# Linear attention and two MLPs in one kernel: keys, values and `q` loaded ahead of most weights, weight conversions in another order, six of them moved from the end of stage one into the slots

## The chip, the core and the metric

The kernel runs on one core of a Trainium2 chip. The metric is the device time of one execution in microseconds (us). Engines: PE is TensorE, DVE VectorE, ACT ScalarE, POOL GpSimd; SP is the queue that issues most DMAs.

## What is computed

A linear attention with RMS normalisation over 8 x 8 heads of 576 tokens, then two MLPs on its 4608 x 512 output, all in float32. The weights arrive as float64 and are read as pairs of 32-bit words.

```python
kv = einsum('bhsd,bhse->bhde', k, v); out = einsum('bhsd,bhde->bhse', q, kv)
x = out / sqrt(mean(out * out, -1) + 1e-6) * g_norm      # then (4608, 512)
x = square(maximum(x @ w_in, 0)) @ w_out                 # moe,  512 -> 2048 -> 512
h = x @ w_in2;  out = (h * cos(h)) @ w_out2              # moe2, 512 -> 2048 -> 512
```

## The kernel before

**Numbers.** A float32 operand is split in a high and a low part (`xh`, `xl`; `wh`, `wl`; `gh`, `gl`), and a product takes three matmuls: high by high, high by low, low by high. ACT rounds the high part, DVE or POOL subtracts it from the value.

**Weights.** `load_w` brings a block of float64 words (512 KB) to SBUF as a tile `raw`, `conv_steps` makes float32 of it. Kind "one" is one block of `w_in` (i = 0) or `w_out` (i = 1) of the first MLP and stays in SBUF as high and low part: six instructions on DVE (L119, L121, L124 in `words`, L130, L133 in `value`, L208) and two on ACT (L120, L207). Kinds "pair" and "seven" take four blocks, add four sums and differences of them in the `raw` tile itself (L177), keep seven, split these (L189 on ACT, L191 on DVE) and write both parts to HBM (`wi_d`, `ws_d`), 448 KB each; only when the second of these DMAs (`wi_d<-raw`, L194) has landed is the `raw` tile free. There are two such tiles (`conv_p`, `bufs=2`); blocks of kind "one" with i = 1 use two tiles of another pool.

**Stage one** takes the first half of the first MLP's 2048 columns in 72 chunks (nine tiles of 512 tokens by eight column blocks f): `layer_in` (L385, 12 matmuls), `act_relu2` (ACT: L394 relu, L395 square, L396 high part; DVE: L397 low part `gl`), and two chunks later `layer_out` (L419, 12 matmuls). Beside it runs the attention: `kv_mm` (L264), `att_a` (L294, L298), `att_b` (L320 and following), `att_c` and `att_d` on DVE, up to chunk 49. The first two batches' attention goes straight into the tiles of the first chunks. Chunks 0 and 1 need the blocks (0, 0) and (1, 0); chunk f needs (f, 0), and its `layer_out` (f, 1).

**The slots**, 30 of them, follow stage one. A slot is one tile of up to 1024 tokens by one group of column blocks: ten slots (0 to 9) for the rest of the first MLP, twenty for the second. They do their products by a scheme of seven block products out of eight (`first_product` L507, `second_product` L669, `second` L606), with weights that the conversions left in HBM (loads `wi`, `ws`, `wo` from SP).

**The order of the side work** is a table of due times, `jobs`, in units of chunks and slots: `at(n, fn, ...)`. `w_items` and `w_at` hold the conversions and when each begins; `Stream.place` spreads a conversion's steps behind its begin (the tuples `steps`, in chunks, or in slots for n of nA0 = 72 and more) and loads a later block when one is done. `pos(s)` is slot s. From chunk 50 to chunk 65 fourteen conversions stand (eight pairs of the first MLP, six of the second), in the slots 1 to 7 another fourteen. A scheduler then orders the instructions on each engine, once, by its own estimates; engines and SP work through their lists in order.

Of the kernel before, what the change touches and what calls it, by code (L numbers as in the profile page):

```python
# [12 lines left out]
AF = mybir.ActivationFunctionType  # L13
ALU = mybir.AluOpType
# [8 lines left out]
def kernel(  # L23
# [15 lines left out]
    nc = tc.nc  # L39
# [3 lines left out]
    NH = NF // 2  # L43
    NP = NH // 2
    NEXACT = 2
    NQ = 3
# [5 lines left out]
    D = 64  # L52
# [17 lines left out]
    gcol = cpool.tile([P, 1], F32, name="gcol")  # L70
# [12 lines left out]
    seven = {(0, 0)} | {(1, q) for q in range(NP)}  # L83
# [20 lines left out]
    def as32(ap):  # L104
        return ap.bitcast(F32)

    def temp(shape, dtype, name):
        return pools["t"].tile(shape, dtype, tag="t", name=name)
# [28 lines left out]
    def load_w(kind, m, f, i):  # L137
        if kind == "seven":
            raw = conv_p.tile([P, 4, P, 2], U32, tag="raw", name="raw")
            for df, places in ((0, (1, 0)), (1, (2, 3))):  # L140
                src = (wA, wB)[m][2 * f + df, :, 1, :].rearrange("p (c n) -> p c n", n=2 * P)
                for d, place in enumerate(places):
                    nc.sync.dma_start(out=raw[:, place].rearrange("p n two -> p (n two)"), in_=src[:, 2 * d + i, :])
        elif kind == "pair":
            raw = conv_p.tile([P, 4, P, 2], U32, tag="raw", name="raw")
            for df, dst in ((0, raw[:, 1:3]), (1, raw[:, 0::3])):
                src = (wA, wB)[m][2 * f + df, :, 0, :].rearrange("p (c n) -> p c n", n=2 * P)
                nc.sync.dma_start(out=dst.rearrange("p k n two -> p k (n two)"), in_=src[:, i::2, :])
        else:
            if kind == "one" and i:  # L150
                raw = x_p.tile([P, DM, 2], U32, tag="xr", name="raw", bufs=2)
            else:
                raw = conv_p.tile([P, DM, 2], U32, tag="raw", name="raw")
            nc.sync.dma_start(out=raw.rearrange("p n two -> p (n two)"), in_=(wA, wB)[m][f, :, i, :])
        raws[kind, m, f, i] = raw
# [123 lines left out]
    def load_q(b, p):  # L279
        t = att_p.tile([P, S], F32, tag="q", name="q", bufs=NQ)  # L280
        nc.sync.dma_start(out=t, in_=qT[p * P:(p + 1) * P, b * S:(b + 1) * S])
        q_sb[b, p] = t
# [89 lines left out]
    gs = {}  # L372
# [3 lines left out]
    def layer_in(t, *fs):  # L376

        pss = [bank("l") for _ in fs]
        for c in range(NKC):
            xh, xl = xs[t, c]  # L380
            cs = slice(c * P, (c + 1) * P)
            for f, ps in zip(fs, pss):
                wh, wl = wts[0, f]
                for k, (a, m) in enumerate(((wh, xh), (wh, xl), (wl, xh))):
                    nc.tensor.matmul(  # L385
                        ps, a[:, 0, cs], m[:], start=(c == 0 and k == 0), stop=(c == NKC - 1 and k == 2)
                    )
        return pss

    def act_relu2(ps):  # L390
        r, g = (temp([P, TOK], F32, n) for n in "rg")
        h = g_p.tile([P, TOK], F32R, tag="gh", name="gh")
        l = g_p.tile([P, TOK], F32R, tag="gl", name="gl")
        nc.scalar.activation(out=r, in_=ps, func=AF.Relu)  # L394
        nc.scalar.activation(out=g, in_=r, func=AF.Square)  # L395
        nc.scalar.copy(out=h, in_=g)  # L396
        nc.vector.tensor_tensor(out=l, in0=g, in1=as32(h[:]), op=ALU.subtract)  # L397
        return h, l
# [307 lines left out]
    chunks = [(t, f) for t in range(NTILE) for f in range(NH)]  # L706
    nA0 = NTILE * NH
    nAtt = 49
# [3 lines left out]
    def at(n, fn, *a):  # L712
        jobs.append((n, len(jobs), fn, a))

    def pos(slot):
        return nA0 + slot + 0.002

    class Stream:
# [10 lines left out]
        def place(self, positions, after, skip=()):  # L729
            for k, (n, item) in enumerate(zip(positions, self.items)):  # L730
                steps = (0, 0.06, 0.13, 0.3, 0.45)
                if n < nA0:
                    steps = (0, 0.25, 0.5, 0.75, 1.0, 1.25, 1.4) if n < nAtt else (0, 0.15, 0.3, 0.5, 1.0)
                if self.use != conv_w or item[0] == "one":
                    at(n, self.use, *item)
                    steps = (after,)
                for d in steps[:-1]:
                    at(n + d, conv_part, *item)
                if k not in skip:
                    at(n + steps[-1], self.advance)  # L740

    def outs_of(m, ps):
        return [("out", m, f, 1) for p in ps for f in (2 * p, 2 * p + 1)]

    def pairs_in(m, ps, kind="pair"):
        return [(kind, m, p, i) for p in ps for i in range(2)]

    w_items, w_at = [], []
    for fs, n, step in ((range(2), -14, 0.1), (range(2, 6), -2.2, 0.7), (range(6, NH), 4, 0.8)):
        new = [("one", 0, f, i) for f in fs for i in range(2)]  # L750
        w_items += new
        w_at += [n + step * k for k in range(len(new))]
    for new, n0, n1 in (
        (pairs_in(0, range(4, 6), "seven") + outs_of(0, range(6, 8)) + pairs_in(1, range(6, 8), "seven") + pairs_in(1, range(4), "seven"), 13, nAtt + 1),
        (pairs_in(0, range(NP, 2 * NP)) + pairs_in(1, range(3)), nAtt + 1, nA0 - 7),
        (pairs_in(1, range(3, 2 * NP)) + pairs_in(1, range(4, 6), "seven"), pos(1), pos(7)),
    ):
        w_items += new
        w_at += [n0 + (n1 - n0) / len(new) * k for k in range(len(new))]
    w_stream = Stream(load_w, conv_w, w_items)  # L760
    w_stream.place(w_at, 0.5, range(2 * NH - NRAW, 2 * NH - NRAW + 2))

# [4 lines left out]
    for b, (s0, ds) in enumerate(starts):  # L767
        for i, u in enumerate(att_units(b)):
            n = s0 + i * ds
# [51 lines left out]
    def run_jobs(n):  # L821
        nonlocal done
        while done < len(jobs) and jobs[done][0] <= n:
            _, _, fn, a = jobs[done]
            done += 1
            fn(*a)

    def run_chunks(lo, hi):
        for n in range(lo, hi):
            if n < LAG:  # L830
                if n == 0:
                    first = layer_in(0, *range(LAG))
                    banks["l"] = ["l0"]
                ps = first[n]
            else:
                ps, = layer_in(*chunks[n])
            gs[chunks[n]] = act_relu2(ps)
            run_jobs(n)
            if n >= LAG:
                layer_out(*chunks[n - LAG])  # L840
            run_jobs(n + 0.5)
# [40 lines left out]
        run_jobs(here)  # L882

    for j in range(2):
        nc.sync.dma_start(out=gcol[j * D:(j + 1) * D, :], in_=g_norm.rearrange("(d o) -> d o", o=1))
    nc.vector.memset(epsb, EPS)
    nc.scalar.activation(out=zerob, in_=epsb, func=AF.Abs_reciprocal_sqrt)
    nc.vector.memset(zerob, 0.0)
# [6 lines left out]
    with ExitStack() as early:  # L895
        pools["ps"] = early.enter_context(tc.tile_pool(name="ps0", bufs=1, space=PSUM))
        def right(name, bufs):
            return early.enter_context(tc.tile_pool(name=name, bufs=bufs, side="right"))

        right("pad", 1).tile([P, 56], F32, name="pad")  # L900
        x_p, g_p, ev_p, pools["t"] = (right(n, b) for n, b in (("x", XB), ("g", 3), ("ev", 2), ("tmp", 8)))
        with tc.tile_pool(name="att", bufs=1, side="right") as att_p:
            kvx = [att_p.tile([P, NKC, P], F32, tag=f"kvx{b}", name=f"kvx{b}") for b in range(2)]
            for x in kvx:
                nc.gpsimd.memset(x, 0.0)
            w_stream.advance(2)
            kv_stream.advance(KVB)
            w_stream.advance(NRAW - 2)
            for p in range(NQ):
                load_q(0, p)  # L910
            run_jobs(-1)
            banks.update(o=["o", "l1"], ss=["ss"], l=["l0", "acc3"])
            run_chunks(0, nAtt)
        pools["x"] = ctx.enter_context(tc.tile_pool(name="xb", bufs=13, side="left"))
        banks["l"] = ["l0", "l1", "o", "ss"]
        run_chunks(nAtt, nA0)
        for c in chunks[-LAG:]:
            layer_out(*c)
# [47 lines left out]
```

## Time and profile before

| | us |
|---|---|
| median of 3 runs (1587.4 to 1589.66) | 1588.98 |
| the profiled execution | 1588.0 |
| its span, first to last instruction | 1586.2 |
| PE busy | 1552.5 (98%) |
| DVE busy | 1243.9 (78%) |
| ACT busy | 1073.7 (68%) |

Stage one takes the span up to 507 us, the slots the rest. A busy PE is not a PE at its peak: matmuls overlap, and their ends are modelled. Matmuls of 128 x 512 that follow each other without a wait start 0.23 us apart, and each is shown as some 0.39 us long. Where PE waits for short times or its clock is lowered, the number of matmuls in a window shows it better than the busy time. A row of a table of windows reads: begin and end, length, busy us (instructions) of PE, of PEld (weight loads), DVE, ACT and POOL, granted TensorE clock, busy share of the 16 DMA engines, GB/s. In a timeline a row reads: start, us, engine, line, instruction, its tiles, shapes, and in brackets the engine's idle time before it and what ended it.

### The profile page before, as it was taken

How to read it: one execution, taken by the hardware profiler on the slowest of the kernel's cores; microseconds unless marked ns; L12 is line 12 of the kernel's file. 1: busy time of each engine (PE TensorE's matmuls, PEld its weight loads, DVE VectorE, ACT ScalarE, POOL GpSimd, SP SyncE). 2: the span in 40 equal slices, each digit the busy share in tenths (PEclk: the TensorE clock that was granted, in tenths of full speed). 3: DMA queues.
4: the chain of work that ended last, by engine and by line, in shares of the span. 5: the costliest groups of instructions: out<-in, count | busy, mean ns of one | idle time of the engine just before them, and what ended most of it. 6: DMA issues, size and time to landing. Idle time of an engine off the chain costs nothing.

```text
span 1586.2 us, 24792 instructions
## 1 busy us (share of the span) xinstructions
PE 1552.5 (98%) x9164; PEld 1359.8 (86%) x9164; DVE 1243.9 (78%) x1688; ACT 1073.7 (68%) x1535; POOL 116.4 (7%) x125
## 2 busy tenths in 40 slices
PE   5999999999989999999999999999999999999998
PEld 4777777778777878888999899999999999999998
DVE  7977868798766798888747678967896788689677
ACT  5977768775545755555636667776777677777774
POOL 1100211111100000000000000000000001100110
PEclk9999999999999999999999999999999999999999
DMA  8855978777679989999987678988999889999995
GB/s 320 276 157 163 279 225 248 217 212 225 213 221 333 320 263 340 312 345 304 339 273 288 231 215 270 269 260 262 268 264 280 239 259 287 279 365 308 265 363 170
DMA packets 236951, 425.53 MB, mean 268 GB/s; under 512 B 18464, under 2 KB 155168, under 8 KB 236832
## 3 DMA queue, kind: packets, MB, share of 16 engines
q1 hardware_dynamic: 225840, 387.78, 72.9%
q0 software_dynamic: 10992, 36.18, 11.3%
q8 instruction: 73, 1.20, 0.3%
q14 instruction: 46, 0.38, 0.1%
HBM read 309.85 MB, written 80.22 MB: 246 GB/s over the span
## 4 chain that ended last, share of the span: by engine, by line
PE 83%; DVE 6%; DMA 5%; issue 3%; ACT 2%; SPq 0%; POOL 0%; DVEq 0%; ACTq 0%; POOLq 0%
PE FA L507 15%; PE FB L507 15%; PE SA L669 13%; PE SB L669 12%; PE acc L419 9%; PE l L385 9%; PE SB L606 3%; PE SA L606 3%; DMA wi_d<-raw 1%; DMA raw<-in_wB 1%; DMA sum<-part 1%; DMA q<-in_qT 1%; DVE raw L177 1%; ACT wh L189 1%; DMA raw<-in_wA 1%
## 5 line engine op out<-in xcount | busy, mean ns | idle before, releaser
L507 PE MATMUL FA<-xh,wi 128*128 128x512 f32 (+1 forms) x840 | 306.1, 370 | 1.1 <-ACT ev L405 0.9
L507 PE MATMUL FB<-xh,wi 128*128 128x512 f32 (+1 forms) x840 | 306.1, 370 | 0.0
L669 PE MATMUL SB<-ws,gh 128*128 128x256 f32 x1008 | 237.9, 280 | 1.1 <-ACT u L521 0.8
L669 PE MATMUL SA<-ws,gh 128*128 128x256 f32 x1008 | 237.9, 280 | 0.0
L669 PEld LDWEIGHTS SB<-ws,gh 128*128 128x128 f32 x1008 | 185.9, 188 | 14.4 <-ACT u L521 1.0
L669 PEld LDWEIGHTS SA<-ws,gh 128*128 128x128 f32 x1008 | 186.2, 188 | 13.2
L507 PEld LDWEIGHTS FA<-xh,wi 128*128 128x128 f32 x840 | 157.8, 188 | 11.0 <-ACT ev L405 1.3
L507 PEld LDWEIGHTS FB<-xh,wi 128*128 128x128 f32 x840 | 157.8, 188 | 8.2
L646 DVE TENSOR_TENSOR gl<-y,gh 128x1024 fp32r<-128x1024 f32 (+1 forms) x100 | 111.4, 1114 | 39.1 <-ACT gh L645 38.9
L669 PE MATMUL SA<-ws,gl 128*128 128x256 f32 x504 | 141.0, 280 | 1.1 <-DVE gl L646 1.1
L669 PE MATMUL SB<-ws,gl 128*128 128x256 f32 x504 | 141.2, 280 | 0.8 <-DVE gl L646 0.8
L695 POOL DMA_DIRECT2D sum<-part x71 | 60.3, 850 | 1100.8 <-ACT part L694 1082.2
L566 DVE SCALAR_TENSOR_TENSOR y<-y,h 128x1024 f32<-128x1024 f32 (+1 forms) x80 | 89.2, 1115 | 53.6 <-ACT y L562 53.2
L548 ACT ACTIVATE y<-h,zerob 128x1024 int32<-128x1024 f32 (+1 forms) x80 | 85.1, 1064 | 50.7 <-DVE h L527 50.7
L419 PE MATMUL acc<-gh,wh 128*128 128x512 f32 x288 | 114.5, 399 | 4.2 <-ACT gh L396 2.5
L419 PE MATMUL acc<-gl,wh 128*128 128x512 f32 x288 | 114.4, 397 | 2.1 <-DVE gl L397 2.1
L419 PE MATMUL acc<-gh,wl 128*128 128x512 f32 x288 | 113.6, 395 | 0.0
L507 PE MATMUL FA<-xl,wi 128*128 128x512 f32 (+1 forms) x300 | 111.0, 370 | 0.0
L507 PE MATMUL FB<-xl,wi 128*128 128x512 f32 (+1 forms) x300 | 110.9, 370 | 0.0
L669 PEld LDWEIGHTS SB<-ws,gl 128*128 128x128 f32 x504 | 94.7, 188 | 7.9 <-DVE gl L646 1.5
L669 PEld LDWEIGHTS SA<-ws,gl 128*128 128x128 f32 x504 | 94.7, 188 | 7.8 <-DVE gl L646 1.3
L645 ACT CAST gh<-y 128x1024 fp32r<-128x1024 f32 (+1 forms) x100 | 94.5, 957 | 6.1 <-DVE y L628 6.0
(178 smaller groups left out, 3781.6 us busy)
## 6 DMA issues: line engine op xcount, KB each, us to landing
wi<-wi_d SPq DMA_DIRECT2D x210, 512.0 KB, 6.9
ws<-ws_d SPq DMA_DIRECT2D x175, 512.0 KB, 5.8
sum<-part POOLq DMA_DIRECT2D x45, 512.0 KB, 7.7
kvld<-in_kv SPq DMA_DIRECT2D x32, 512.0 KB, 6.9
wi_d<-wh SPq DMA_DIRECT2D x24, 448.0 KB, 4.1
wi_d<-raw SPq DMA_DIRECT2D x24, 448.0 KB, 4.0
raw<-in_wA SPq DMA_DIRECT2D x20, 512.0 KB, 5.5
wo<-wo_d SPq DMA_DIRECT2D x20, 512.0 KB, 6.4
```

The source lines that it names most:

```text
L177: nc.vector.tensor_tensor(out=a[:, o], in0=a[:, x], in1=a[:, y], op=op)
L189: nc.scalar.copy(out=h, in_=a[:, lo:end])
L385: nc.tensor.matmul(ps, a[:, 0, cs], m[:], start=(c == 0 and k == 0), stop=(c == NKC - 1 and k == 2))
L419: nc.tensor.matmul(o, a[:, cs], m[:], start=(f == 0 and n == 0), stop=(f == NH - 1 and n == 2), skip_group_check=True)
L507: nc.tensor.matmul(ps[:, pp, :], a, b, start=(i in (0, 1, 2) and n == 0), stop=(n == 5), skip_group_check=True)
L548: nc.scalar.activation(out=y.bitcast(I32), in_=hs[k, b], func=AF.Identity, bias=zerob)
L566: nc.vector.scalar_tensor_tensor(out=y, in0=y, scalar=-2.0 * math.pi, in1=hs.pop((k, b)), op0=ALU.add, op1=ALU.mult)
L606: nc.tensor.matmul(ps, lhs, rhs, start=(a == 0 and (x, y) == (0, 0)), stop=last, skip_group_check=True)
L645: nc.scalar.copy(out=h, in_=src)
L646: nc.vector.tensor_tensor(out=l, in0=src, in1=as32(h), op=ALU.subtract)
L669: nc.tensor.matmul(ps[:, b, :], lhs, rhs, start=(i in (0, 1, 2) and n == 0 and (m == 0 or b % 2 == 0)), stop=(n == 5), skip_group_check=True,)
L695: nc.gpsimd.dma_start(out=e, in_=part, accum_op=ALU.add)
```

## The change

- `g_norm` is loaded by POOL's queue, not by SP's. SP's first loads are one weight block, the five blocks of keys and values of batch 0, `q` of the first head pair, and then weights and `q` in turn; before, two weight blocks came first and two more ahead of all `q`.
- The sixteen blocks of kind "one" are converted in another order: (0, 0), (1, 0), (2, 0), (0, 1) ahead of the first chunk, then block (f, 0) 3.4 chunks and block (f, 1) 0.7 chunks ahead of chunk f. Before: 0 to 3, both halves in turn, ahead of the first chunk, then 4 to 7.
- Six conversions (the first three pairs of the second MLP) move from the end of stage one to the slots, where twenty now stand from slot 1 to slot 9.2. Those that stay have their steps 0.25 chunks apart, over 1.4 chunks in all, before over 1.0.
- From chunk 49 on the square of `act_relu2` is made by DVE from PSUM, max(ps, 0) times the relu, not by ACT.

```diff
             else:
-            if kind == "one" and i:
+            if kind == "one" and w_items.index((kind, m, f, i)) % 4 > 1:
                 raw = x_p.tile([P, DM, 2], U32, tag="xr", name="raw", bufs=2)
...
-    def act_relu2(ps):
+    def act_relu2(ps, busy):
...
-        nc.scalar.activation(out=g, in_=r, func=AF.Square)
+        if busy:
+            nc.scalar.activation(out=g, in_=r, func=AF.Square)
+        else:
+            nc.vector.scalar_tensor_tensor(out=g, in0=ps, scalar=0.0, in1=r, op0=ALU.max, op1=ALU.mult)
...
                 if n < nA0:
-                    steps = (0, 0.25, 0.5, 0.75, 1.0, 1.25, 1.4) if n < nAtt else (0, 0.15, 0.3, 0.5, 1.0)
+                    steps = (0, 0.25, 0.5, 0.75, 1.0, 1.25, 1.4)
...
-    for fs, n, step in ((range(2), -14, 0.1), (range(2, 6), -2.2, 0.7), (range(6, NH), 4, 0.8)):
-        new = [("one", 0, f, i) for f in fs for i in range(2)]
-        w_items += new
-        w_at += [n + step * k for k in range(len(new))]
+    ones_at = {(0, 0): -14, (1, 0): -13.9, (2, 0): -4, (0, 1): -3}
+    for f in range(NH):
+        ones_at.setdefault((f, 0), f - 3.4 if f > 2 else 0)
+        ones_at.setdefault((f, 1), f - 0.7)
+    for (f, i), n in sorted(ones_at.items(), key=lambda x: x[1]):
+        w_items.append(("one", 0, f, i))
+        w_at.append(n)
...
-        (pairs_in(0, range(NP, 2 * NP)) + pairs_in(1, range(3)), nAtt + 1, nA0 - 7),
-        (pairs_in(1, range(3, 2 * NP)) + pairs_in(1, range(4, 6), "seven"), pos(1), pos(7)),
+        (pairs_in(0, range(NP, 2 * NP)), nAtt + 1, nA0 - 7),
+        (pairs_in(1, range(2 * NP)) + pairs_in(1, range(4, 6), "seven"), pos(1), pos(9.2)),
...
-            gs[chunks[n]] = act_relu2(ps)
+            gs[chunks[n]] = act_relu2(ps, n < nAtt)
...
-        nc.sync.dma_start(out=gcol[j * D:(j + 1) * D, :], in_=g_norm.rearrange("(d o) -> d o", o=1))
+        nc.gpsimd.dma_start(out=gcol[j * D:(j + 1) * D, :], in_=g_norm.rearrange("(d o) -> d o", o=1))
...
-            w_stream.advance(2)
+            w_stream.advance(1)
             kv_stream.advance(KVB)
+            load_q(0, 0)
+            w_stream.advance(1)
+            load_q(0, 1)
             w_stream.advance(NRAW - 2)
-            for p in range(NQ):
-                load_q(0, p)
+            load_q(0, 2)
```

In the orders below line numbers of the changed kernel differ: `gl` is L400 there (before L397), the moved square L398.

SP at the program's start, before (`raw` are weight blocks, `kvld` keys and values):

```order
L885 DMA gcol<-in_g_norm 64x1 x2
L154 DMA raw<-in_wA 128x1024 x2
L252 DMA kvld<-in_kv 128x1024 x4
L252 DMA kvld<-in_kv 64x1024
L154 DMA raw<-in_wA 128x1024 x2
L281 DMA q<-in_qT 128x576 x3
```

SP at the same place, now:

```order
L154 DMA raw<-in_wA 128x1024
L252 DMA kvld<-in_kv 128x1024 x4
L252 DMA kvld<-in_kv 64x1024
L281 DMA q<-in_qT 128x576
L154 DMA raw<-in_wA 128x1024
L281 DMA q<-in_qT 128x576
L154 DMA raw<-in_wA 128x1024 x2
L281 DMA q<-in_qT 128x576
```

`gcol` and the second weight block have left the place ahead of the keys and values, and the first `q` stands right behind these.

DVE from the fourth conversion's first instruction to the first instruction of attention, L335, before:

```order
L119 TENSOR_SCALAR e<-raw 128x512
L133 SCALAR_TENSOR_TENSOR w<-w,e 128x512
L121 TENSOR_SCALAR w<-raw 128x512
L130 SCALAR_TENSOR_TENSOR e<-raw,e 128x512
L208 TENSOR_TENSOR wl<-w,wh 128x512
L124 SCALAR_TENSOR_TENSOR w<-raw,w 128x512
L133 SCALAR_TENSOR_TENSOR w<-w,e 128x512
L119 TENSOR_SCALAR e<-raw 128x512
L335 SCALAR_TENSOR_TENSOR m<-ss,r_311 128x288
```

DVE from the second conversion's first instruction to the first instruction of attention, now:

```order
L119 TENSOR_SCALAR e<-raw 128x512
L121 TENSOR_SCALAR w<-raw 128x512
L124 SCALAR_TENSOR_TENSOR w<-raw,w 128x512
L130 SCALAR_TENSOR_TENSOR e<-raw,e 128x512
L133 SCALAR_TENSOR_TENSOR w<-w,e 128x512
L335 SCALAR_TENSOR_TENSOR m<-ss,r_287 128x288
```

Ahead of attention's first instruction stood four conversions, the last one still without its L208, and the beginning of a fifth; now there are two, the second without its L208.

DVE near the end of stage one, one conversion and the `gl` around it, before:

```order
L397 TENSOR_TENSOR gl<-g,gh 128x512
L191 TENSOR_TENSOR raw<-raw,wh 128x896
L119 TENSOR_SCALAR e<-raw 128x512
L121 TENSOR_SCALAR w<-raw 128x512
L124 SCALAR_TENSOR_TENSOR w<-raw,w 128x512
L130 SCALAR_TENSOR_TENSOR e<-raw,e 128x512
L133 SCALAR_TENSOR_TENSOR raw<-w,e 128x512
L177 TENSOR_TENSOR raw<-raw 128x128 x4
L397 TENSOR_TENSOR gl<-g,gh 128x512
L191 TENSOR_TENSOR raw<-raw,wh 128x896
```

DVE at the same place, now:

```order
L400 TENSOR_TENSOR gl<-g,gh 128x512
L398 SCALAR_TENSOR_TENSOR g<-l_4888,r 128x512
L119 TENSOR_SCALAR e<-raw 128x512
L121 TENSOR_SCALAR w<-raw 128x512
L400 TENSOR_TENSOR gl<-g,gh 128x512
L124 SCALAR_TENSOR_TENSOR w<-raw,w 128x512
L130 SCALAR_TENSOR_TENSOR e<-raw,e 128x512
L133 SCALAR_TENSOR_TENSOR raw<-w,e 128x512
L177 TENSOR_TENSOR raw<-raw 128x128 x4
L398 SCALAR_TENSOR_TENSOR g<-o,r 128x512
L191 TENSOR_TENSOR raw<-raw,wh 128x896
L400 TENSOR_TENSOR gl<-g,gh 128x512
```

A conversion now spans two `gl` where it spanned one, and each chunk's square stands on DVE as well.

## Rows read from the trace of the kernel before

**Rows 1.** The page, part 1: busy us, share of the span, instructions.

```profile
PE 1552.5 (98%) x9164; PEld 1359.8 (86%) x9164; DVE 1243.9 (78%) x1688; ACT 1073.7 (68%) x1535; POOL 116.4 (7%) x125
```

**Rows 2.** Windows, end of stage one: length, busy us (count) by engine, clock, DMA.

```profile
360.00:400.00 40.00, 40.00 (x178) 33.10 (x178) 32.37 (x64) 23.27 (x39) 4.02 (x3) 1.00 0.72 220
400.00:440.00 40.00, 38.33 (x168) 30.96 (x167) 31.29 (x60) 20.64 (x34) 4.56 (x3) 1.00 0.69 213
440.00:480.00 40.00, 35.40 (x142) 27.68 (x141) 29.27 (x60) 21.15 (x33) 0.00 (x0) 0.91 0.80 245
```

**Rows 3.** Timeline of PE, 455 to 483 us: start, us, instruction [idle before, releaser].

```profile
467.58 0.79 PE L419 MATMUL acc<-gl,wh 128*128 128x512 f32 x1 [1.43 <-DVE gl L397]
```

**Rows 4.** Timeline of DVE, 465 to 478 us.

```profile
471.93 0.43 DVE L119 TENSOR_SCALAR e<-raw 128x512 uint32<-128x512 uint32 x1 [3.61 <-DMA raw<-in_wB]
...
475.67 0.69 DVE L397 TENSOR_TENSOR gl<-g,gh 128x512 fp32r<-128x512 f32 x1
```

**Rows 5.** Chain of waits, 395 to 485 us: start, us, what.

```profile
426.10 3.22 DMA wi_d<-raw
...
429.76 3.43 DMA raw<-in_wB
...
439.77 3.21 DMA wi_d<-raw
```

**Rows 6.** Timeline of SP at the start.

```profile
0.74 1.23 SPq L885 DMA_DIRECT2D gcol<-in_g_norm  x2
```

**Rows 7.** Timeline of PE at the start.

```profile
18.54 2.26 PE L294 MATMUL acc<-q,kvx 128*128 128x288 f32 x4 [1.79 <-DMA q<-in_qT]
```

**Rows 8.** Windows of the start.

```profile
0.00:25.00 25.00, 11.88 (x97) 9.07 (x98) 14.60 (x34) 10.59 (x22) 1.19 (x6) 1.00 0.88 322
...
50.00:95.00 45.00, 44.77 (x274) 34.15 (x273) 44.77 (x98) 38.71 (x87) 4.22 (x7) 1.00 0.67 217
```

**Rows 9.** Windows, instructions of DVE on tile `raw` alone (then clock, DMA share, GB/s).

```profile
400.00:440.00 40.00, 26.97 (x52) 1.00 0.69 213
```

**Rows 10.** Windows of slots: 6 to 9, ten us, slots 9, 3, 7, 10.

```profile
720.90:848.20 127.30, 127.30 (x694) 121.78 (x693) 90.17 (x106) 69.44 (x86) 0.00 (x0) 1.00 0.91 318
770.00:780.00 10.00, 10.00 (x60) 10.00 (x59) 10.00 (x12) 7.08 (x10) 0.00 (x0) 1.00 1.03 403
818.50:848.20 29.70, 29.70 (x174) 29.70 (x173) 26.28 (x28) 20.29 (x25) 0.00 (x0) 1.00 1.00 369
601.50:641.10 39.60, 39.01 (x173) 31.98 (x172) 37.21 (x39) 26.71 (x29) 0.00 (x0) 1.00 0.99 339
...
756.60:787.70 31.10, 31.10 (x172) 29.99 (x171) 26.57 (x30) 18.84 (x25) 0.00 (x0) 1.00 0.94 352
...
848.20:884.40 36.20, 36.20 (x178) 32.15 (x177) 21.93 (x21) 18.73 (x19) 0.00 (x0) 1.00 0.67 218
```

**Rows 11.** DMA issues: tiles, count, KB each, median us to landing.

```profile
wi_d<-wh SPq DMA_DIRECT2D x24, 448.0 KB, 4.1
wi_d<-raw SPq DMA_DIRECT2D x24, 448.0 KB, 4.0
...
raw<-in_wB SPq DMA_DIRECT2D x32, 256.0 KB, 3.5
```

**Rows 12.** Tile `x_d`, 20 to 60 us, stored by POOL.

```profile
DMA to landing us min/median/max: 2.0/5.4/7.2
```

**Rows 13.** Timeline of DVE, 76 to 104 us.

```profile
81.34 0.69 DVE L397 TENSOR_TENSOR gl<-g,gh 128x512 fp32r<-128x512 f32 x1
...
83.62 0.43 DVE L121 TENSOR_SCALAR w<-raw 128x512 uint32<-128x512 uint32 x1
...
84.59 0.68 DVE L124 SCALAR_TENSOR_TENSOR w<-raw,w 128x512 uint32<-128x512 uint32 x1
85.19 0.69 DVE L130 SCALAR_TENSOR_TENSOR e<-raw,e 128x512 uint32<-128x512 uint32 x1
```

**Rows 14.** Timeline of PE, 85 to 87.5 us: chunk 5's second product begins.

```profile
86.52 0.39 PE L419 MATMUL acc<-gh,wh 128*128 128x512 f32 x1
```

## The prediction

> **What bounds the kernel now.** TensorE is busy for 98% of the span [rows 1], so only what it loses counts. I read three stages: the start (to about 100 us), the end of stage one (400 to 507 us), the slots behind it.
>
> The end of stage one first, by the table of windows. Three windows of 40 us hold 178, 168 and 142 matmuls, and PE is called busy in nearly all of each; the count tells more than the busy time [rows 2]. Against twice the first, 46 are missing, at 40/178 = 0.225 us each: **10.3 us lost**. PE's timeline shows where: 1.43 us for the `gl` of one chunk, for example [rows 3]. Such waits come from VectorE: its L119, the first instruction of a conversion, stands 3.61 us waiting for its `raw` load, and the next `gl`, at 475.67, is queued behind it [rows 4]. Why the load is late is told by the chain of waits: the output of one conversion leaves its `raw` buffer from 426.10 on, the next load into that buffer runs from 429.76 on, and that buffer's next output starts at 439.77 [rows 5]. One turn is 13.67 us and there are two buffers, so conversions can't follow each other closer than 6.8 us. The planner wants 14 of them in 15 chunks of 24 matmuls, 15 x 5.4 = 81 us, one in 5.8 us. The lag grows until it reaches PE. Part of the loss is TensorE's clock: its grant falls to 0.91 in the last window [rows 2].
>
> The start: SP issues `gcol` for 1.23 us before the first weight load [rows 6]; PE begins attention at 18.54, after waiting 1.79 us for `q` [rows 7]. VectorE stands idle 10.4 of the first 25 us and then works 44.77 of 45 us from 50 to 95, PE as much [rows 8]: both are full there.
>
> In slots 6 to 9 PE is busy for the whole 127.30 us [rows 10]; there is nothing to win there, only to lose.
>
> **The change, part by part.**
>
> *Six conversions leave the end of stage one.* Eight remain in 15 chunks, one in 10.1 us. Their steps are spread wider, 1.4 chunks instead of 1.0, which adds 0.4 x 5.4 = 2.2 us to a turn: 15.9 us, or 7.9 us for each conversion, and 10.1 is above it. So L119 should find its load landed and `gl` stays in time. A square per chunk moves from ScalarE to VectorE, 23 in all; bounded by the 0.69 us of a `gl` [rows 4], which has the same number of columns (the square reads PSUM where `gl` reads SBUF; no row shows this form at that width). Per chunk VectorE then has 2 x 0.69 plus 5.4/10.1 of a conversion, and one conversion costs it 5.2 us (26.97 us over 52 instructions, ten each) [rows 9]. That is 4.2 of 5.4 us. ScalarE only loses work. The worst case is that squares stand behind a conversion's pieces so long that nothing is won. I take **-10.0 us** and leave 0.3 us of stalls; bounds -10.3 and 0.
>
> *They go to the slots.* By the order of the built program VectorE begins two more in slot 6, one more in slot 7 and three more in slot 8; slots 1 to 5 stay as they are but for single steps. Slots 6 to 9 were 127.3 us in which VectorE worked 90.17 [rows 10]; with 6 x 5.2 it is 121.4, or 95%. In slot 3 it works 37.21 of 39.6 us, 94%, and PE loses 0.6 us [rows 10]. The DMA engines are the greater risk. A conversion moves 512 KB in and twice 448 KB out [rows 11], 1.44 MB; six are 8.7 MB on top of 318 GB/s x 127.3 us = 40.5 MB [rows 10]. 49.1 MB in 127.3 us is 386 GB/s. The best 10 us there carried 403, slot 9 carried 369 with the engines' share at 1.00, both with PE busy throughout [rows 10]. At 403 the extra is hidden; at 369 it takes 133.1 us, 5.8 more, of which the loads' lead over their use can hide some. By shares it looks worse: 213 GB/s took a share of 0.69 where conversions were nearly all the traffic [rows 9], so one takes 1.44/8.5 x 0.69 x 40 = 4.7 us of all engines, six 28 us, and only 0.09 x 127.3 = 11.5 us are free: 16.7 us over. Bounds 0 and 16.7; I take **+2.0 us**, a third of the 5.8 from the row nearest in kind, since a late load hurts only once its lead is gone.
>
> The Trainium skill ("DMA: Bandwidth & Descriptors", section "Where 436 GB/s comes from") states that for transfers between HBM and SBUF the HBM side binds, at about 358 GB/s for a core. An estimate by that page: 49.1 MB would take 137.2 us, 9.9 more than the slots have. The rows with 403 and 369 GB/s speak against it as a hard ceiling.
>
> *The start.* `gcol` moves to POOL's queue, so the first weight load is issued 1.23 us sooner. The row nearest in kind, POOL's stores of `x_d`, lands between 2.0 and 7.2 us after its issue [rows 12]; `gcol` heads VectorE's queue, so the first conversion may start anywhere from on time to about 4 us late. That costs nothing, because VectorE's second conversion has to wait for a load that now comes behind all of `kvld`. The second weight block (0.52 MB) no longer precedes `kvld`: at the 322 GB/s of this stretch [rows 8] 1.6 us. With most of the wait for `q` gone too, attention can start some 3 us sooner, near 15.4. In exchange VectorE has two conversions less to do while it waits, and PE's later needs decide. By the order, what the second product of chunk 5 needs (its `gl` and its half of `w_out`) has 14 conversions ahead of it on VectorE, before 12. Four instructions of a conversion last 0.68 and start 0.60 apart; the two short ones last 0.43, so some 0.35 apart [rows 13]: 3.1 us each, 6.2 for two, and with 0.7 us of other work that moved ahead too 6.9 us. Before, that `gl` ended at 82.03 [rows 13] and PE took it at 86.52 [rows 14], a lead of 4.5 us. So PE gets to this point 2.4 us later if VectorE's idle time stays what it is. The sooner attention can shrink that idle time by at most 3 us: -0.6 to 2.4. Standing without the two conversions can lengthen it: 2 us more give +4.5. I take **+1.0 us**; bounds -3 (attention's whole lead comes through) and +4.5.
>
> Sum, against the profiled execution's 1588.0 us (a span of 1586.2 and 1.8 around it; the median of the three runs is 1.0 above it, inside their spread): 1588.0 - 10.0 + 2.0 + 1.0 = **1581.0 us**.
>
> **The rivals.**
>
> 1. *The slots become bound by DMA.* Place: slots 6 to 9, where `wi`, `ws` and `wo` queue on SP behind `raw` loads and conversion outputs. Price by shares: +16.7 us instead of +2.0, so 1595.7, slower. It turns the change into a loss once the engines carry less than 49.1/136.3 = 360 GB/s there (9.0 us over). For it: the share of 1.00 at 369. Against it: the 403, and the 218 GB/s of slot 10 [rows 10], in which a backlog can drain.
> 2. *A milder ceiling.* The two fullest slots carried 352 and 369 GB/s [rows 10]; if their mean, 360, is all there is, the same loads are late by 8.9 us: 1587.9, no change. The page on DMA named above has such a ceiling as its rule.
> 3. *The start gains what it is meant to.* Attention 3 us sooner and no stall at chunk 5: -3 instead of +1, 1577.0. For it: PE's waits up to there are for loads [rows 7]. Against it: VectorE is full from 50 on [rows 8].
> 4. *The end of stage one keeps its stalls.* Then conversions were paced by VectorE's queue, which now has a second pass for each chunk: 1591.0 with the two other terms. Against it: L119 waits there for a load, by name [rows 4].
>
> **How the numbers follow.** Forecast (1578 to 1585.5) 0.58; rival 3 0.20; rival 2 and lesser forms of rivals 1 and 4, within 0.2%, 0.15; slower through rival 1 or rival 4 in full 0.07. Two tenths of a per cent is 3.2 us, about what a measurement of this kernel can tell from no change. So faster 0.78, same 0.15, slower 0.07. The range takes in rival 3 and most of the cases without change: 1575.5 to 1588.
>
> **What would show it.** Windows 400 to 440 and 440 to 480 with 175 matmuls or more each and no wait of PE for `gl` show the first term; if L119 still waits there for `raw`, it was wrong. In slots 6 to 9 (about 10 us sooner) idle time of PE with `wi` or `ws` as releaser shows rival 1; their sum should be 127 to 131 us. At the start: attention's first matmul near 15.4, VectorE still full from 50 to 95, and chunk 5's second product near 88 show my term; if that stands near 83, rival 3 holds. The prediction fails if the stretch from the first slot on is longer by more than 5 us.

## The result and the profile after

| | us |
|---|---|
| changed kernel, median of 6 runs (1598.99 to 1605.12) | 1602.38 |
| kernel before, median of the runs beside it (1585.21 to 1589.7) | 1588.19 |
| ratio, 95% interval | 1.0092 [1.008, 1.0103] |
| profiled execution after, its span | 1599.0, 1597.2 |

The change makes the kernel slower by 14 us, where 7 us less were forecast. The profiled execution is the fastest of its runs; against the profiled one of before its span is 11.0 us longer, and the sections below place these 11.0 us.

Part 1 of the page after, beside [rows 1]: TensorE does the same instructions and is busy 4 us longer; the other 7 us are idle time of PE.

```profile
PE 1556.5 (97%) x9164; PEld 1362.1 (85%) x9164; DVE 1258.7 (79%) x1711; ACT 1060.1 (66%) x1512; POOL 116.7 (7%) x127
```

A table made from PE's timelines places them: the begin of chunk 9's second product, of slot 0, of slot 6 and of slot 10.

| | before | after | later by |
|---|---|---|---|
| chunk 9's second product | 118.5 | 127.9 | 9.4 |
| slot 0 | 507.1 | 506.4 | -0.7 |
| slot 6 | 720.9 | 719.4 | -1.5 |
| slot 10 | 848.2 | 860.8 | 12.6 |
| end of the span | 1586.2 | 1597.2 | 11.0 |

The first row rests on these two lines, before and after:

```profile
118.50 0.50 PE L419 MATMUL acc<-gh,wh 128*128 128x512 f32 x1
```

```profile
127.86 0.50 PE L422 MATMUL acc<-gh,wh 128*128 128x512 f32 x1
```

So the start loses 9.4 us, the end of stage one gains 10.1, slots 6 to 9 lose 14.1 (141.4 for 127.3), the rest gains 2.4. These 2.4 us (0.8 ahead of slot 6, 1.6 behind slot 10) were not looked into.

**End of stage one,** windows after (columns as in [rows 2]):

```profile
360.00:400.00 40.00, 40.00 (x179) 33.19 (x178) 29.89 (x62) 20.26 (x38) 5.56 (x4) 1.00 0.65 199
400.00:440.00 40.00, 40.00 (x178) 33.12 (x177) 33.60 (x59) 18.44 (x29) 4.30 (x3) 1.00 0.56 171
440.00:480.00 40.00, 40.00 (x178) 33.15 (x177) 29.25 (x46) 16.32 (x24) 0.00 (x0) 1.00 0.70 218
```

178 matmuls in each of the last two windows, where [rows 2] had 168 and 142; the granted clock stays at 1.00. PE waits for nothing from 360 to 505, and VectorE's L119 once for a `raw` load, for 0.6 us.

**The start.** VectorE's timeline: `gcol` and the first two weight conversions, then PE's with attention's first matmul.

```profile
8.93 0.15 DVE L899 TENSOR_SCALAR gcol<-gcol 128x1 f32<-128x1 f32 x1 [6.57 <-DMA gcol<-in_g_norm]
9.00 0.42 DVE L119 TENSOR_SCALAR e<-raw 128x512 uint32<-128x512 uint32 x1
...
15.86 0.43 DVE L119 TENSOR_SCALAR e<-raw 128x512 uint32<-128x512 uint32 x1 [2.68 <-DMA raw<-in_wA]
```

```profile
16.38 2.26 PE L294 MATMUL acc<-q,kvx 128*128 128x288 f32 x4 [0.95 <-issue]
```

Attention begins 2.2 us sooner than in [rows 7]. Two windows of after beside [rows 8], and one more:

```profile
0.00:25.00 25.00, 13.26 (x100) 9.37 (x100) 9.95 (x26) 10.05 (x23) 3.00 (x9) 1.00 0.89 320
...
50.00:95.00 45.00, 38.38 (x227) 27.95 (x226) 44.81 (x96) 34.83 (x77) 3.46 (x6) 0.93 0.66 218
90.00:100.00 10.00, 10.00 (x32) 7.18 (x32) 8.19 (x18) 6.68 (x14) 0.00 (x0) 0.72 0.35 98
```

In the first 25 us VectorE works 9.95 us for 14.60. From 50 to 95 it is full in both kernels, but PE does 227 matmuls for 274. PE's waits from 50 to 100 us, 6.5 us together, name attention's `m` on VectorE (3.3) and ScalarE (3.2); before, they were 0.2 us.

**Slots 6 to 9,** their sum, then slots 7, 8 and 9, beside [rows 10]:

```profile
719.40:860.80 141.40, 131.34 (x698) 124.06 (x697) 118.69 (x167) 75.53 (x96) 0.00 (x0) 0.99 0.97 337
755.90:789.60 33.70, 32.75 (x180) 31.36 (x179) 29.80 (x39) 20.00 (x27) 0.00 (x0) 1.00 1.00 346
789.60:821.70 32.10, 29.93 (x171) 29.20 (x170) 27.97 (x46) 16.99 (x23) 0.00 (x0) 1.00 0.96 307
821.70:860.80 39.10, 32.16 (x173) 31.26 (x173) 29.46 (x31) 21.05 (x27) 0.00 (x0) 0.96 1.04 385
```

The DMA engines are busy for 0.97 of 141.4 us, that is 137 us, where they were for 0.91 of 127.30, 116 us [rows 10]; VectorE is at 84%. The longest wait of PE there, with what stands ahead of it on ScalarE, VectorE and SP:

```profile
843.00 0.56 PE L672 MATMUL SA<-gh,ws 128*128 128x384 f32 x1 [4.66 <-issue]
```

```profile
838.38 0.81 ACT L524 ACTIVATE m<-FA 128x768 f32<-128x768 f32 x1 [2.11 <-PE FA L510]
839.09 0.82 ACT L648 CAST gh<-h 128x768 fp32r<-128x768 f32 x1
```

```profile
839.94 0.96 DVE L649 TENSOR_TENSOR gl<-h,gh 128x768 fp32r<-128x768 f32 x1 [2.68 <-ACT gh L648]
840.82 1.22 DVE L460 TENSOR_TENSOR xt<-xraw 128x1024 f32<-128x1024 f32 x1
841.95 0.95 DVE L700 TENSOR_TENSOR sum<-SA,sum 128x768 f32<-128x768 f32 x1
```

```profile
828.11 4.11 SPq L489 DMA_DIRECT2D ws<-ws_d  x1
...
837.93 0.49 SPq L484 DMA_DIRECT2D wi<-wi_d  x1
```

SA, a tile of PSUM into which PE adds up, is drained at 841.95 by an instruction that stands on VectorE behind `gl` and `xt`. No load is named as the releaser. What points to the transfers is SP: one issue takes 4.11 us, another 10 us later 0.49. Which cause it is, the trace alone can't say; runs have to.

### The profile page after: what moved, and what is told of

It is laid out like the page before. It is cut to its first block, busy times and chain, and to the rows that moved or that the text cites. A ratio compares the mean times of both kernels' runs of the same rounds, so it can differ in the third digit from the quotient of the medians.

```text
span 1597.2 us, 24806 instructions
## 1 busy us (share of the span) xinstructions
PE 1556.5 (97%) x9164; PEld 1362.1 (85%) x9164; DVE 1258.7 (79%) x1711; ACT 1060.1 (66%) x1512; POOL 116.7 (7%) x127
## 4 chain that ended last, share of the span: by engine, by line
PE 85%; DVE 5%; DMA 4%; ACT 3%; issue 2%; SPq 0%; POOL 0%; DVEq 0%; ACTq 0%; POOLq 0%
PE FB L510 16%; PE FA L510 16%; PE SA L672 14%; PE SB L672 13%; PE acc L422 9%; PE l L385 8%; PE SA L609 3%; PE SB L609 3%; DMA x_d<-xo 1%; PE o L385 1%; PE ss L385 1%; DMA kvld<-in_kv 1%; DMA wi_d<-raw 1%; DMA xraw<-x_d 1%; DVE w L124 1%
## 5 line engine op out<-in xcount | busy, mean ns | idle before, releaser
L510 PEld LDWEIGHTS FA<-xh,wi 128*128 128x128 f32 x840 | 157.7, 188 | 14.1 <-ACT m L524 4.3
L385 PE MATMUL l<-xh,wh 128*128 128x512 f32 x240 | 98.5, 410 | 3.2 <-ACT r L394 2.3
```

The source lines that it names most:

```text
L385: nc.tensor.matmul(ps, a[:, 0, cs], m[:], start=(c == 0 and k == 0), stop=(c == NKC - 1 and k == 2))
L510: nc.tensor.matmul(ps[:, pp, :], a, b, start=(i in (0, 1, 2) and n == 0), stop=(n == 5), skip_group_check=True)
```

## The experiments

All are compared with the kernel before in the runs beside them. The table holds medians, ratios, chunk 9's second product (us), and slots 6 to 9 (us).

| kernel | us | ratio, 95% interval | chunk 9 | slots 6 to 9 |
|---|---|---|---|---|
| changed | 1602.4 | 1.0092 [1.008, 1.0103] | 127.9 | 141.4 |
| start_old | 1592.8 | 1.0032 [1.0021, 1.0043] | 117.6 | 144.0 |
| gcol_sp | 1603.0 | 1.009 [1.0075, 1.0105] | 131.4 | 141.4 |
| six_back | 1603.8 | 1.0093 [1.0072, 1.0115] | 128.8 | 127.3 |
| spread | 1580.2 | 0.9943 [0.9927, 0.996] | 117.8 | 129.5 |
| order_only | 1603.5 | 1.0089 [1.0065, 1.0114] | 126.9 | 144.5 |
| loads_only | 1595.7 | 1.005 [1.0033, 1.0066] | 121.8 | 142.5 |
| no_out2 | 1582.6 | 0.9967 [0.9951, 0.9982] | 118.0 | 132.6 |
| no_dve2 | 1594.3 | 1.0025 [1.0011, 1.004] | 117.6 | 144.0 |
| order_early | 1593.4 | 1.0033 [1.0017, 1.005] | 118.3 | 143.5 |
| spread_plain | 1581.3 | 0.9958 [0.9944, 0.9972] | 117.6 | 129.8 |
| best | 1581.7 | 0.9963 [0.9951, 0.9975] | 118.4 | 128.1 |

**start_old: the start as before.** The edit puts back the old loads, `gcol` on SP, and the old order of the sixteen first conversions with their old due times and tiles. Shown in part:

```diff
-        nc.gpsimd.dma_start(out=gcol[j * D:(j + 1) * D, :], ...
+        nc.sync.dma_start(out=gcol[j * D:(j + 1) * D, :], ...
...
-    ones_at = {(0, 0): -14, (1, 0): -13.9, (2, 0): -4, (0, 1): -3}
...
+    for fs, n, step in ((range(2), -14, 0.1), (range(2, 6), -2.2, 0.7), (range(6, NH), 4, 0.8)):
...
-            w_stream.advance(1)
+            w_stream.advance(2)
             kv_stream.advance(KVB)
```

> The changed kernel with the start as it was before (gcol on SP, two weight blocks ahead of keys and values, the old order of the sixteen first conversions); the rest of the change stays. Theory A, the start and the slots lose separately: the start gives back the 9.3 us by which chunk 9's second product came later (127.9 for 118.5), so 1602.4 - 9.3 = 1593; slots 6 to 9 stay near 141 us and the end of stage one has no stalls. Theory B, a later start is made up by shorter waits in the slots, so undoing it gives nothing there: 1600 to 1603, with slots 6 to 9 near 150. Whoever holds that the start was harmless expects 1602.

Measured 1592.8: theory A to the microsecond. The whole 9.6 us of the start comes back, so the two losses are separate in the main; slots 6 to 9 take 144.0 us here, 2.6 more than in the changed kernel.

**gcol_sp: only `gcol` back on SP's queue.**

> The changed kernel with one line undone: gcol is loaded by SP's queue ahead of everything, as before. Theory A, gcol's late landing on POOL's queue (VectorE waits 6.57 us for it, 1.44 before) is a part of what the start lost: the first conversion begins near 6 to 7 instead of 9.0, chunk 5's second product comes 3 to 5 us sooner than 96.4, the time is 1598. Theory B, VectorE's idle time behind it is set by the second weight block (15.86) anyway, so only the order of the conversions counts: chunk 5 within 1 us of 96.4, 1602.

1603.0, and nothing comes sooner: theory B by its cause. Its number for chunk 5 was missed: 99.95, 3.6 us later than in the changed kernel, and chunk 9 is 3.5 later. The two profiled executions differ by about as much in all (1603.0 and 1599.0), and the changed kernel's runs go from 1599.0 to 1605.1, so this difference is not put down to the edit. The first conversion begins at 7.00 in that run, but the second at 16.53, when its load lands; the late `gcol` is covered, as the prediction said.

**order_only and loads_only: the two halves of the new start.** Each leaves one of them as before.

> The changed kernel with the first loads as before (gcol on SP, two weight blocks ahead of keys and values): of the new start only the order of the conversions is left. It stands against start_old (1592.8) and the changed kernel (1602.4). Theory A, the start lost by two things of which neither alone passes chunk 5's lead of 4.5 us by much: two more conversions ahead of chunk 5 (6.2 to 6.9 us of VectorE) and VectorE's longer idle time before its second conversion (4.8 us less work in the first 20 us). Then the order alone costs 6.9 - 4.5 = 2.4 us: 1595. Theory B, the order is all of it: 1602. Theory C, the loads are all of it: 1593.

> The changed kernel with the old order of the sixteen first conversions, but the new order of the first loads, gcol on POOL's queue too. Theory A (both, over a lead of 4.5 us): VectorE's 4.8 to 6.3 us of idle time less the lead, so 0.3 to 1.8 us on top of 1592.8: 1593 to 1595. Theory B (the order is all): 1593. Theory C (the loads are all): 1602.

The new order with its due times costs all of it (1603.5, 1.5 us above theory B's number), the new loads alone 2.8 us (0.7 above theory A's range), both together no more than the order. Theory A's price for the order, 2.4 us, was far off. VectorE's timeline in order_only shows where it went:

```profile
29.12 0.69 DVE L208 TENSOR_TENSOR wl<-w,wh 128x512 fp32r<-128x512 f32 x1
...
38.96 0.46 DVE L335 SCALAR_TENSOR_TENSOR m<-ss,r 128x288 f32<-128x288 f32 x1 [2.07 <-ACT r L327]
...
47.61 0.46 DVE L337 TENSOR_TENSOR xo<-m,og 128x288 f32<-128x288 f32 x1 [1.92 <-DMA x_d<-xo]
47.99 0.42 DVE L119 TENSOR_SCALAR e<-raw 128x512 uint32<-128x512 uint32 x1
```

The fourth conversion ends at 29.8 and the fifth begins at 47.99. Between them stands attention alone, a chain in which VectorE waits again and again. In start_old two conversions stand among the same instructions and fill those gaps. Windows 30 to 50 of start_old, then of order_only (VectorE is the third engine):

```profile
30.00:40.00 10.00, 8.19 (x97) 6.51 (x97) 9.48 (x23) 7.95 (x22) 1.86 (x4) 0.86 0.87 315
40.00:50.00 10.00, 9.61 (x41) 7.15 (x40) 9.04 (x22) 9.94 (x26) 1.62 (x3) 1.00 1.02 353
```

```profile
30.00:40.00 10.00, 9.71 (x102) 7.71 (x103) 6.68 (x20) 8.01 (x24) 1.88 (x4) 0.84 0.69 249
40.00:50.00 10.00, 9.67 (x42) 7.53 (x41) 7.30 (x19) 7.86 (x23) 2.16 (x4) 1.00 1.00 367
```

18.52 us of work for 13.98: 4.5 us lost, ahead of a stretch in which VectorE has none to spare.

The changed kernel has another course: its third and fourth conversions stand between 22 and 40 us, the fifth begins at 46.45, and VectorE loses more in the first 30 us (15.0 of work, in start_old 19.6) than from 30 to 50 (16.0, in start_old 18.5):

```profile
30.00:40.00 10.00, 9.91 (x86) 6.83 (x84) 8.44 (x21) 6.93 (x20) 1.61 (x3) 0.79 0.60 214
40.00:50.00 10.00, 9.22 (x39) 7.18 (x39) 7.54 (x20) 8.95 (x25) 2.16 (x4) 1.00 1.02 357
```

VectorE's work in the first 50 us and the begin of chunk 5's second product, in us (order_early follows below):

| kernel | VectorE's work, 0 to 50 | chunk 5 |
|---|---|---|
| start_old | 38.1 | 85.7 |
| order_early | 37.4 | 88.9 |
| loads_only | 33.2 | 89.9 |
| order_only | 31.9 | 95.4 |
| changed | 30.9 | 96.4 |

From 50 to 85 VectorE is full in all five (34.9 or more of 35 us). In loads_only, order_only and the changed kernel chunk 5 is later than in start_old by the work that VectorE lost, and in the last two by the 3.2 us of order_early on top, to within 0.7 us.

**order_early: the new order, due when the conversions were due before.**

```diff
-    for (f, i), n in sorted(ones_at.items(), key=lambda x: x[1]):
+    early = [-14, -13.9, -13.8, -13.7] + [-2.2 + 0.7 * k for k in range(8)] + [4 + 0.8 * k for k in range(4)]
+    for ((f, i), _), n in zip(sorted(ones_at.items(), key=lambda x: x[1]), early):
```

> As order_only (first loads as before, the new order of the sixteen first conversions, the rest of the change), but the sixteen begin at the due times of before: four ahead of everything, eight from 2.2 chunks ahead of chunk 0 on, 0.7 apart, four from chunk 4 on. In order_only no conversion ran on VectorE from 29.8 to 48.0 us (the fifth was due at -0.4), in start_old two did. Theory A, the due times cost the 10 us, not the order: 1592.8 again, or up to 3 us less, and chunk 9's second product near 117.6. Theory B, the order as such (two more conversions ahead of chunk 5): 1600 to 1603, chunk 9 near 126.9.

1593.4, chunk 9 at 118.3: theory A. With the same order and the old loads the start loses nothing; the loss of order_only was in the due times. The third and fourth conversion begin as early in both (16.9 and 19.3 us in order_only, 17.1 and 19.4 here), whatever their due times; the fifth to the twelfth are due 0.6 to 1.8 chunks later in order_only, and the fifth, at -0.4 instead of -2.2, begins at 47.99 instead of 23.21. The two more conversions ahead of chunk 5 do show there (88.9 for 85.7 in start_old), and are made good by chunk 9. The old due times with the new loads were run in loads_only alone, with the old order.

**six_back: the six conversions back at the end of stage one.**

```diff
-        (pairs_in(0, range(NP, 2 * NP)), nAtt + 1, nA0 - 7),
-        (pairs_in(1, range(2 * NP)) + pairs_in(1, range(4, 6), "seven"), pos(1), pos(9.2)),
+        (pairs_in(0, range(NP, 2 * NP)) + pairs_in(1, range(3)), nAtt + 1, nA0 - 7),
+        (pairs_in(1, range(3, 2 * NP)) + pairs_in(1, range(4, 6), "seven"), pos(1), pos(7)),
```

> The changed kernel with the six conversions back at the end of stage one (14 there, 14 in the slots up to slot 7); the square on VectorE, the wider steps and the new start stay. Theory A, the six conversions alone made slots 6 to 9 longer: their sum is back at 127 to 128 us for 141.4, the end of stage one loses its 10 us again, 1602.4 - 14 + 10 = 1598. Theory B, the slots lose by something else (the later phase of the program, a queue): the sum stays near 141 and the time rises to 1612.

Slots 6 to 9 are back at 127.3, as theory A says. The time is neither theory's: the stretch from chunk 48's second product to slot 0 takes 138.4 us, 14.8 more than in the changed kernel (123.6), where before lost 10.5 (134.1). Fourteen conversions with the wider steps and the square on VectorE are worse than without; the turn of 15.9 us, or 7.9 for each conversion, that the prediction worked out for the wider steps points that way, as their outputs `wi_d<-raw` leave 8.1 us apart on average there (fourteen from 392.19 to 498.10), but the two edits were not tried apart.

**no_out2 and no_dve2: transfers or VectorE?** Both start from start_old and change the last six conversions only. The first writes 128 KB of each instead of 896, and reads other weights in their place.

```diff
+                if late(kind, m, f, i):
+                    h, end = h[:, :1], lo + 1
                 nc.sync.dma_start(out=dst[:, lo - 1:end - 1, 0, :], in_=as32(h))
-            nc.sync.dma_start(out=dst[:, :, 1, :], in_=as32(l[:, 1:]))
+            n = 1 if late(kind, m, f, i) else NPR
+            nc.sync.dma_start(out=dst[:, :n, 1, :], in_=as32(l[:, 1:1 + n]))
```

> The kernel with the start of before and all twenty conversions in the slots as in the change (start_old; slots 6 to 9 take 144.0 us there), but the last six conversions write one of their seven products for each of the two parts instead of seven, 128 KB instead of 896 KB (the loads that would read the rest read another group's weights, so the result differs); VectorE's and ScalarE's work stays. Theory A, the DMA engines bind in slots 6 to 9: 6 x 0.77 = 4.6 MB less of 48.96 MB (340 GB/s x 144.0), 44.4 MB at 347 GB/s (340 at a share of 0.98) is 128 us, so slots 6 to 9 take 127.3 to 131 us, the time is 1577 to 1581. Theory B, VectorE's queue binds, since it has as much to do: 140 us or more, 1590.

The second keeps all transfers and cuts VectorE's part.

```diff
+            if late(kind, m, f, i):
+                w = temp([P, 4, P], U32, "w")
+                nc.vector.tensor_scalar(out=w, in0=raw[..., 1], scalar1=0x3FFFFFFF, scalar2=None, op0=ALU.bitwise_and)
+            else:
+                w, e = words(raw, [P, 4, P])
...
+                n = lo + 1 if late(kind, m, f, i) else end
+                nc.vector.tensor_tensor(out=l[:, lo:n], in0=a[:, lo:n], in1=as32(h[:, :n - lo]), op=ALU.subtract)
```

> The same kernel (start_old) with all the transfers of the last six conversions, but with VectorE's part of them cut from 5.2 to some 1.4 us each (one instruction instead of five makes the words, and the low part is formed for one of seven products, so the result differs): 23 us less of VectorE's 118.4 in slots 6 to 9. Theory A, the DMA engines bind: slots 6 to 9 stay within 3 us of 144.0, 1590 to 1593. Theory B, VectorE's queue binds: 127 to 132 us, 1577 to 1581.

Slots 6 to 9 as windows, of start_old, no_out2 and no_dve2:

```profile
710.90:854.90 144.00, 133.94 (x698) 126.69 (x697) 118.43 (x167) 75.51 (x96) 0.00 (x0) 0.96 0.98 340
```

```profile
711.40:844.00 132.60, 129.82 (x698) 122.36 (x698) 115.71 (x165) 75.34 (x96) 0.00 (x0) 1.00 0.91 323
```

```profile
710.00:854.00 144.00, 133.29 (x697) 126.71 (x696) 101.00 (x144) 75.30 (x95) 0.00 (x0) 0.96 0.97 339
```

With 17.4 us less work on VectorE nothing changes; with 4.6 MB less to write, and VectorE as busy as ever, 11.4 us come back. Theory A both times, though 132.6 is 1.6 us above what I gave it, and the two times, 1582.6 and 1594.3, are 1.6 and 1.3 above. One thing is not told apart: the scheduler's estimates take the transfers in, so the order on PE, VectorE and ScalarE differs a little between these kernels, and part of the loss may have passed through that order.

**spread: the twenty conversions placed by room.** It starts from start_old.

```diff
-        w_at += [n0 + (n1 - n0) / len(new) * k for k in range(len(new))]
+        w_at += [pos(1 + 5 / 12 * k) for k in range(12)] + [pos(6.2 + 0.95 * k) for k in range(4)] + [pos(10 + 0.45 * k) for k in range(4)] if n0 > nA0 else [n0 + (n1 - n0) / len(new) * k for k in range(len(new))]
```

> The kernel with the start of before, and the twenty conversions in the slots placed unevenly: twelve in slots 1 to 5, four in slots 6 to 9 instead of eight, four in slots 10 and 11, where the DMA engines had a share of 0.67. Theory A, the engines' time is what slots 6 to 9 lack (a conversion takes 4.7 us of all sixteen, 11.5 us were free, so two more than before fit): slots 6 to 9 take 127 to 130 us, the time is 1593 - 13 = 1580. Theory B, any conversion there beyond the old two costs PE its share of time through VectorE's or SP's queue: 141.4 - 4/6 of 14 = 132 us, 1584, or, if slots 10 and 11 then lose as much, 1590 to 1593.

1580.2 us, 0.9943 of before (0.6% less) and the shortest time of all: theory A. Windows of slots 6 to 9, of slot 10 and of slot 11:

```profile
711.10:840.60 129.50, 128.50 (x698) 122.39 (x696) 102.70 (x136) 71.69 (x91) 0.00 (x0) 1.00 0.91 316
840.60:876.70 36.10, 36.10 (x177) 32.17 (x178) 31.94 (x44) 23.15 (x26) 0.00 (x0) 1.00 0.89 315
876.70:915.30 38.60, 38.60 (x236) 34.85 (x235) 31.30 (x33) 27.78 (x30) 0.91 (x1) 1.00 1.00 342
```

The same slots 10 and 11 in start_old, without conversions:

```profile
854.90:891.00 36.10, 36.10 (x178) 32.10 (x177) 19.04 (x18) 18.49 (x19) 0.00 (x0) 1.00 0.65 214
891.00:929.60 38.60, 38.60 (x236) 34.85 (x236) 27.84 (x24) 26.52 (x28) 0.93 (x2) 1.00 0.65 225
```

They take the same 36.10 and 38.60 us with four conversions as with none: their engines had the time free.

**spread_plain and best: what else counts?** The first drops the square on VectorE and the wider steps, the second adds order_early's start.

> The kernel spread without the two edits that go with the move: the square is made by ScalarE throughout, and the conversions at the end of stage one have their old steps, over 1.0 chunks. What is left of the change is the move of six conversions, with the uneven places in the slots. Theory A, the two buffers bind at the end of stage one and eight conversions in fifteen chunks are enough to free it: 1580 within 1 us, no stall there. Theory B, VectorE's queue has to be spread too (six_back, with both edits and fourteen conversions, lost 16.0 us there for 10.3 before, so they count): stalls of 1 us or more there, 1582 to 1585, or, if the square on VectorE only costs, 1578.

> The kernel spread with the sixteen first conversions in the new order at the due times of before (as in order_early). Theory A (due times): 1577 to 1580.5. Theory B (order): 1588 to 1590.

Both lie within 1.5 us of spread, and the spread of their runs (1578.2 to 1582.0 and 1578.8 to 1586.1) covers it. In spread_plain 179 and 178 matmuls stand in the windows 400 to 440 and 440 to 480: the move of the six alone freed the end of stage one, the other two edits were not needed for it. Theory A is the nearer one both times, with 0.3 and 1.2 us above what I gave it. The new order at the old times brings nothing that can be measured.

## Why the prediction was wrong, step by step

Two steps failed: the rate of the DMA engines in slots 6 to 9 (12.1 us) and VectorE's idle time in the start (8.4 us). Less 0.1 us of the first term and 2.4 of the rest, which the sum had at nothing, they lead from 1581.0 to the profiled 1599.0. From slot 0 on the program is 11.7 us longer, more than the 5 that I had named as the sign of being wrong.

- **End of stage one, -10.0: right.** -10.1, no wait of PE, and no need of the companion edits (spread_plain). That fits the two buffers' turn; what the turn and VectorE's own work each cost was not tried apart.
- **Slots 6 to 9, +2.0: the step that failed most.** Measured +14.1, inside its bounds of 0 and 16.7, so the choice between the ends was wrong, not the ends. The need was close (49.1 MB forecast, 141.4 us x 337 GB/s = 47.7 MB moved). The rate was not: I took 369 to 403 GB/s from two windows [rows 10], and the engines carried 337 over the stretch at a share of 0.97, 347 when full. The window of ten us and the one slot said what the engines carry in a good moment; with more conversions among the loads they carry less (traffic that was nearly all conversions had 213 GB/s at a share of 0.69 [rows 9], 309 if full). The term by shares, 4.7 us of all engines for a conversion, I had called worse-looking and set aside: it gave 16.7, and start_old shows 0.98 x 144.0 = 141 us of engine time for 116 before, 25 us for six, 4.2 each. The same price placed `spread` right: two conversions more than before fit into the 11.5 us that were free in these slots. So rival 1 came true in kind, with a chance of 0.07 that it shared with rival 4; the time lies above its 1595.7 because the start failed too.
- The page that I cited ("DMA: Bandwidth & Descriptors" of the Trainium skill, section "Where 436 GB/s comes from") gave, as an estimate, 9.9 us more by its 358 GB/s. By direction this case agrees with it; the 347 measured is lower still, while slot 9 of the changed kernel carried 385 for 39.1 us.
- **The sign I had named for it did not show.** I said that PE's idle time would name `wi` or `ws`; the trace names ScalarE, VectorE and "issue". The windows' share and SP's issue of 4.11 us pointed to it, and no_out2 and no_dve2 bore it out.
- **The start, +1.0 between -3 and +4.5: outside the bounds, +9.4.** I priced the order by counting conversions ahead of chunk 5 and let VectorE's idle time grow by 2 us at most (2.4 and 2 make 4.4, not 4.5, which changes nothing). The count was about right (2.4 forecast; order_early: 3.2 us later at chunk 5), and cost nothing in the end. What failed is the idle time: by 50 us VectorE had done 6.5 us less than before (30.9 for 37.5), 4.7 of it in the first 25, and chunk 5's second product, which I had put near 88, came at 96.40. Two things made it idle. The new loads cost VectorE 4.9 us of work against start_old (loads_only), and the later due times 6.1 (order_only, where they left it alone with attention from 29.8 to 48.0); together they cost it 7.1. The sign "VectorE still full from 50 to 95" held (44.81) and was worthless, since the loss lay ahead of it.
- Two lesser points held: `gcol`'s late landing costs nothing, and attention's first matmul came sooner (16.38; I said 15.4), without bringing the first chunk's second product sooner (52.89, before 52.53).

## What to carry to other kernels

Work that fills gaps in another chain is worth the gaps: when it is moved later, price the idle time that it leaves, not only the place it has in the queue. Room for transfers is to be counted in busy time of the DMA engines, by the share that the same kind of traffic takes elsewhere in the trace, and not by the best rate that some window reached. Where a stretch is full, put the moved work by room, slot by slot, in place of an even spread.

## What I had not expected of the hardware

TensorE's granted clock fell where PE waited for VectorE: in the changed kernel PE lost 6.6 of the 45 us from 50 to 95, and the clock was 0.72 from 90 to 100. PE had waited 0.95 and 1.89 us for attention's `m`, up to 87.29 and 89.71. Matmuls of the same shape, without waits, at 94 and at 97 us:

```profile
94.47 0.63 PE L385 MATMUL l<-xh,wh 128*128 128x512 f32 x1
94.89 0.63 PE L385 MATMUL l<-xl,wh 128*128 128x512 f32 x1
...
97.20 0.40 PE L385 MATMUL l<-xh,wh 128*128 128x512 f32 x1
97.43 0.39 PE L385 MATMUL l<-xl,wh 128*128 128x512 f32 x1
```

They start 0.42 us apart and then 0.23, the lower and the upper of the clock's two levels (1.2 and 2.4 GHz). So this stall was paid for twice, by the wait and by the matmuls behind it: the twelve from 90.46 on took 5.3 us, where 0.23 each is 2.8, and only 32 matmuls stand in the 10 us from 90 on.
